# Attention and a two-layer MLP on one core: two jobs with P in float32 in place of four, four x blocks by TensorE in place of two, and products planned behind the landing

## The chip, the core and the metric

The program runs on one core of a Trainium2 chip. The metric is its time on the device in microseconds (us): 715.67 for the kernel before, the median of three runs (715.53 to 716.65). The core has TensorE (PE; its weight loads are shown apart as PEld), VectorE (DVE), ScalarE (ACT), GpSimd (POOL), and SyncE (SP), whose queue issues the DMAs here. Each engine takes its own instructions strictly in the order in which they were written down, and waits on semaphores for the others.

## The reference

Attention with pooled queries, whose output goes as tokens through a two-layer MLP (cut to what matters):

```python
# q, k, v: (4, 8, 1152, 64); w_in: (512, 2048); w_out: (2048, 512); float32
q_pool = q.reshape(B, H, S // 2, 2, D).mean(axis=3)            # 576 queries
scores = (1.0 / np.sqrt(D)) * np.matmul(q_pool, k.transpose(0, 1, 3, 2))
scores = scores - np.max(scores, axis=-1, keepdims=True)
attn = np.exp(scores)
attn = attn / (np.sum(attn, axis=-1, keepdims=True) + 1e-09)
x = np.matmul(attn, v)                       # tokens: (2304, 512) after the heads are joined
h = x @ w_in
g = h * (1.0 / (1.0 + np.exp(-h)))
return (g @ w_out).astype(np.float32)
```

## The kernel before

*Jobs.* The 32 heads are 16 pairs, four pairs to a batch. A job is one pair and one chunk of 128 queries; the 64 queries left over of two pairs make one job too. That gives 72 jobs, counted here from 0; each has two sides, one per head. Jobs 0 to 3 are the first chunk of the first four pairs. The first four pairs keep q and k in float32 (18 jobs); for the others each operand is split into two float16 halves, high and low, and a product is three: high by high, high by low, low by high.

*One job.* PE makes the scores into the PSUM tiles S0 and S1, one pair of them for all jobs, so that the next job's scores wait until both exponentials have read them (`scores`). For each side DVE takes the row maximum (L786, L793) and ACT the exponential P with its sum (L802). The usual way on: a cast to the high half (ACT or DVE, tile `phl`), the low half by a subtraction (DVE or POOL, L434), and a transpose of each half by DMA through SP's queue into `pt` (L829). Then PE multiplies P and V: 27 products a side into `po` (L937), and DVE divides by the sum into `x32` (L1009).

*Sides with P in float32* (`by_32`, the first `SIDES32` sides, so jobs 0 to 3): PE transposes P itself by nine transposes a side into PSUM (L879), ACT or DVE copies it out (L689), and the product is taken in float32 (`po<-ld,pt`, L925: 9 matmuls a side, two passes each). There is no split of P and no DMA. A third way, not used before, is `turn` (`by_pe`): the same nine transposes, then a copy to the high half and a subtraction on DVE to the low half, both out of PSUM, and products in float16.

*Token blocks.* When the four pairs of a chunk are done, `rows` turns x into columns: a split and a DMA transpose, or, for the first `X_BY_PE` blocks, four PE transposes (L1066) and a copy and a subtraction out of PSUM. 18 blocks of 128 tokens go through the MLP: 192 first products of 128 columns (L1132), tanh on ACT, gate on DVE, split on ACT and POOL, 48 second products of 512 columns (L1227; L1180 in the last block), and a store.

*Weights.* They arrive in float64 and are turned into two float16 halves in 32 pieces while the first jobs run: per piece one ACT step L608, a step on bits (L615 on ACT or L621 on DVE), a join on DVE (L636), casts and a subtraction (tiles `w1`, `w2`).

*What sets the order.* A planner (`Plan.order`) runs before anything is emitted. It steps through a model of the five queues with a cost for each operation, takes for a free engine the ready operation with the smallest number (job number plus a term from the tables `PRI`, `PRE`, `W`, `EV`), and holds back what has no tile free. `ready_at` says when an operation's inputs are there. The order that comes out is fixed in the program. Spare matmuls on a constant (`spin`, L1277) are put into gaps of PE at the start.

Of the kernel before, what the change touches and what calls it, by code (L numbers as in the profile page):

```python
# [50 lines left out]
W_OUT_SCALE = 2.0**8  # L51
SUM_GUARD = 1e-9 * math.exp(P_SHIFT)

WAIT = 0.2
AHEAD, SWITCH, STEAL = 5.072, 896.315, 0.782
PREP_LEAD = -3.124
FIRST_LEAD, FIRST_STEP = 5.48, 7.653
W_FIRST, W_STEP, W2_LATER = -3.911, 1.281, -1.06
V_LATER, V_FIRST = 1231.981, 5959.774
PRI = dict(  # L60
    score=-4011.901, top=0.206, exp=-0.93, hi=4.18, lo=0.019, turn=-5.094, flip=8248.55,
    flat=-82.007, sums=-470.427, rows=-218.032, side=0.01, load=-11.832, raw=-5.743,
    xturn=-4252.055,
)
PRE = dict(
    score=-50.801, top=-4.429, exp=1.476, hi=2.474, lo=-45.251, turn=-8.317, sums=-24.354,
    side=-5.025,
)
W = dict(
    t=1.782, low=2.528, put=-72655.385, more=3.2, hi=-5.024, lo=-4.185,  # L70
)
EV = dict(
    x=12.863, xh=12.347, xl=35.706, px=23.928, tanh=-54.817, gate=-8.882, ghi=-226.385, glo=-20.279,
    osb=8.238,
)
SOON = 8
BUFS = dict(w=1, slots=4, b=13, m=17, x4=1, small=3, S=1, mm=2)
# [1 line left out]
SPARE_B = 1  # L79
RAW_ROOM, LOAD_ROOM, P32_ROOM, PHL_ROOM = 2, 4, 1, 1  # L80
PIECES = 4, 2
BOTH_BY_PE, ONE_BY_PE, EVERY = 0, 0, 99


F32_PAIRS = 4
# [16 lines left out]
MORE = True  # L102
SUM_BY_PE = False
VC = D + 2 if SUM_BY_PE else D
X_BY_PE = 2
SIDES32 = 8
LAST = B * FULL + B // 2 - 1


# [33 lines left out]
class Plan:  # L143
# [29 lines left out]
    def ready_at(self, op, engine):  # L173
        at = 0.0
        for b in op.before:
            same = b.engine == engine and engine not in ("dve", "dma")
            at = max(at, b.end + (0.0 if same else LATENCY[b.engine]))
        return at + (DMA_START if engine == "dma" else 0.0)

    def order(self):  # L180
# [162 lines left out]
def dve_cost(n, fast=False):  # L343
    return 0.06 + n * (0.00053 if fast else 0.00105)
# [18 lines left out]
def tile_kernel(tc, q, k, v, w_in, w_out, out):  # L363
    nc = tc.nc
    with ExitStack() as ctx:
# [76 lines left out]
        low, high = slice(0, 64), slice(64, 128)  # L442
# [109 lines left out]
        def weights(n):  # L552
# [67 lines left out]
            def low_on(engine):  # L620
# [4 lines left out]

            ways = {
                "act": ("act", act_cost(512) + 0.02, low_act),
                "dve": ("dve", dve_cost(512, True), low_on(nc.vector)),
            }
            either(  # L630
                [ways[x] for x in LOW_BY],
# [311 lines left out]
        def finish(j):  # L943
# [15 lines left out]
            for i, (pp, col) in enumerate(sides(j)):  # L959
                pt = st["pt"][i]  # L960
                keep = col * P
                if ch is None:
                    hs, parts = (0, 1), ((low, (low, high)[i]), (high, (high, low)[i]))
                else:
                    hs, parts = (col,), ((whole, whole),)
                tokens = [x for n in range(2) for x in pt_tokens(j, n)]
                if by_32(j, i):
                    add(
                        "pe", 9 * 4 * pe_cost(64) + 0.1,
                        lambda pt=pt, pp=pp, hs=hs, keep=keep: heads(  # L970
                            po(), whole32(pt), None, hs, None, keep, v32s[pp]()
                        ),
                        j + pri(j, "sums"), [*tokens, ("ld", pp, "v")],
                        [("po", j)], [po, pt, v32s[pp], x32], matmuls=18,
                    )
                    continue
                add(
                    "pe", 0.787 if len(hs) == 1 else 0.86,
                    lambda pt=pt, pp=pp, hs=hs, parts=parts, keep=keep: heads(
                        po(), pt(), vt[pp](), hs, parts, keep  # L980
                    ),
                    j + pri(j, "sums"), [*tokens, ("vh", pp), ("vl", pp), ("one", pp)],
                    [("po", j)], [po, pt, vt[pp], x32], matmuls=27 * len(hs), mode=0 if len(hs) == 1 else 2,
                )
# [349 lines left out]
```

## Time and profile before

| | us |
|---|---|
| median of 3 runs | 715.67 |
| the profiled execution | 716.49 |
| its span | 714.7 |
| PE busy | 678.1 (95%) |
| DVE busy | 553.0 (77%) |
| ACT busy | 464.9 (65%) |
| POOL busy | 304.3 (43%) |

The profile is one execution; its span leaves out 1.79 us around it. Busy shares are means over stages that have different limits, so they are read by stage. Matmuls are pipelined: a group's mean time of one is longer than the distance between two, so PE's costs are taken from rows that show a run of them from start to start. On ACT and DVE neighbouring rows overlap by about a tenth of a microsecond.

### The profile page before, as it was taken

Reading aid. Unit: us, or ns where it says so; the run is one execution under the profiler, and the core shown is the slowest. Engines: PE = TensorE matmul, PEld = TensorE weight load, DVE = VectorE, ACT = ScalarE, POOL = GpSimd, SP = SyncE. Lnnn points to the kernel's source line nnn. Section 1 sums busy time; section 2 is a strip of 40 time slices with the busy share of each in tenths; the row PEclk is TensorE's granted clock in tenths of the full one; section 3 lists DMA queues with packets and bytes.
Section 4 is the critical chain, followed back from the end, with each engine's and each line's share of the span. In section 5 each row is a group of like instructions: output and inputs, shape, how many; then the busy total and the mean of one; then the engine's idle time right before and its main releaser. Section 6 shows DMA issues by size and latency. Waiting matters only on the chain.

```text
span 714.7 us, 23377 instructions
## 1 busy us (share of the span) xinstructions
PE 678.1 (95%) x10128; PEld 492.2 (69%) x10128; DVE 553.0 (77%) x903; ACT 464.9 (65%) x691; POOL 304.3 (43%) x204
## 2 busy tenths in 40 slices
PE   7898879999999999999999999999999999999997
PEld 5666546767656685858576777675867676868767
DVE  5777969898888988988769887779978887895111
ACT  4788887876776665667566667577757675665221
POOL 1637657746727021366420516164544052404111
PEclk9999999999999999999999999999999999999999
DMA  8983799999999998999999899999999999999000
GB/s 344 412 342 72 143 212 198 202 239 215 222 242 193 183 178 153 174 220 200 213 263 159 152 175 178 169 248 202 197 240 191 184 161 187 164 155 160 24 17 16
DMA packets 353416, 135.75 MB, mean 190 GB/s; under 512 B 340641, under 2 KB 340897, under 8 KB 353313
## 3 DMA queue, kind: packets, MB, share of 16 engines
q1 hardware_dynamic: 353152, 134.13, 97.4%
q8 instruction: 79, 1.29, 0.8%
q14 instruction: 25, 0.20, 0.1%
q10 hardware_dynamic: 160, 0.13, 0.1%
HBM read 45.09 MB, written 4.72 MB: 70 GB/s over the span
## 4 chain that ended last, share of the span: by engine, by line
PE 37%; DMA 10%; DVE 9%; ACT 6%; issue 3%; SPq 1%; POOL 0%; ACTq 0%; DVEq 0%
PE mm L1132 14%; PE mm L1227 9%; DMA pt<-phl 8%; PE po L937 7%; PE S L725 6%; DVE nm L786 4%; DVE phl L434 3%; ACT phl L410 2%; ACT p L802 2%; DMA ld<-q 2%; PE mm L1180 1%; ACT t L1146 1%; DMA ld<-v 1%; DMA xt<-xs 0%; DVE t L1153 0%
## 5 line engine op out<-in xcount | busy, mean ns | idle before, releaser
L802 ACT ACTIVATE p<-S,nm 128x1152 f32<-128x1152 f32 x144 | 175.2, 1217 | 93.6 <-DVE nm L793 68.8
L1132 PE MATMUL mm<-xt,w 128*128 128x128 f16 x3456 | 203.0, 219 | 5.0 <-DMA xt<-xs 1.4
L786 DVE TENSOR_REDUCE nm<-S 128x1 f32<-128x1152 f32 x144 | 194.0, 1347 | 14.7 <-PE S L725 14.6
L1132 PEld LDWEIGHTS <-w 128*128 128x128 f16 x3456 | 194.7, 98 | 11.4 <-issue 3.8
L1227 PE MATMUL mm<-w,g 128*128 128x512 f16 x816 | 186.1, 379 | 1.6 <-DVE nm L793 1.0
L434 POOL TENSOR_TENSOR g<-t,g 128x512 f16<-128x512 f32 x71 | 94.0, 1325 | 216.2 <-ACT g L410 187.0
L434 DVE TENSOR_TENSOR phl<-p,phl 128x1152 f16<-128x1152 f32 x96 | 145.5, 1522 | 19.0 <-ACT phl L410 15.3
L725 PE MATMUL S<-K,Q 64*128 64x512 f16 (+7 forms) x1320 | 136.6, 366 | 0.5 <-ACT p L802 0.3
L1227 PEld LDWEIGHTS <-g 128*128 128x128 f16 x816 | 75.9, 98 | 86.0 <-issue 1.2
L937 PE MATMUL po<-V,pt 128*128 128x64 f16 (+1 forms) x4104 | 124.0, 194 | 11.2 <-DMA pt<-phl 6.2
L937 PEld LDWEIGHTS <-pt 128*128 128x128 f16 (+1 forms) x4104 | 115.8, 101 | 23.8 <-issue 8.5
L434 POOL TENSOR_TENSOR phl<-p,phl 128x1152 f16<-128x1152 f32 x40 | 98.0, 2450 | 55.5 <-ACT phl L410 39.0
L410 ACT ACTIVATE phl<-p 128x1152 f16<-128x1152 f32 x85 | 98.3, 1161 | 4.5 <-DMA pt<-phl 2.8
L1153 DVE SCALAR_TENSOR_TENSOR t<-t,mm 128x512 f32<-128x512 f32 x72 | 49.1, 683 | 51.9 <-ACT t L1146 51.3
L725 PEld LDWEIGHTS <-Q 64*128 64x128 f16 (+1 forms) x1080 | 42.7, 96 | 49.4 <-issue 9.2
L1146 ACT ACTIVATE t<-mm 128x512 f32<-128x512 f32 x72 | 42.5, 591 | 24.5 <-PE mm L1132 24.2
L410 ACT ACTIVATE g<-t 128x512 f16<-128x512 f32 x69 | 43.4, 629 | 20.9 <-DVE t L1153 18.7
L414 DVE CAST phl<-p 128x1152 f16<-128x1152 f32 x51 | 43.0, 842 | 9.0 <-ACT p L802 4.3
L434 POOL TENSOR_TENSOR xs<-x,xs 128x512 f16<-128x512 f32 (+1 forms) x18 | 21.1, 1173 | 47.3 <-ACT xs L410 47.2
L725 PEld LDWEIGHTS S<-K,Q 64*128 64x128 f32 (+1 forms) x240 | 22.8, 196 | 25.0 <-issue 21.9
L1009 DVE TENSOR_TENSOR x<-po,r 128x128 f32<-128x128 f32 x72 | 20.5, 284 | 20.8 <-PE po L937 14.2
L410 ACT ACTIVATE t<-mm 128x512 f32<-128x512 f32 (+1 forms) x16 | 9.2, 578 | 30.9 <-PE mm L1227 21.1
(67 smaller groups left out, 472.9 us busy)
## 6 DMA issues: line engine op xcount, KB each, us to landing
ld<-q SPq DMA_DIRECT2D x16, 576.0 KB, 5.3
ld<-v SPq DMA_DIRECT2D x16, 576.0 KB, 5.5
ld<-k SPq DMA_DIRECT2D x12, 576.0 KB, 6.1
pt<-phl SPq DMA_TRANSPOSE x272, 4.2
wide<-w_in SPq DMA_DIRECT2D x8, 512.0 KB, 10.3
wide<-w_out SPq DMA_DIRECT2D x8, 512.0 KB, 10.7
raw<-w_in SPq DMA_DIRECT2D x8, 512.0 KB, 8.3
raw<-w_out SPq DMA_DIRECT2D x8, 512.0 KB, 7.9
```

Of the source, the lines that this page charges most:

```text
L410: nc.scalar.activation(out=out(), in_=src(), func=AF.Copy, scale=scale or 1.0)
L414: nc.vector.tensor_copy(out=out(), in_=src())
L434: return lambda: getattr(engine, op)(out=out(), in0=a(), in1=b())
L725: nc.tensor.matmul(o[to, c], lhsT=a[rows, s], rhs=x[rows, c], start=n == 0, stop=n == len(terms) - 1,)
L786: lambda: nc.vector.tensor_reduce(out=nm(), in_=ps()[:, :S], op=ALU.max, axis=AX.X),
L802: lambda: nc.scalar.activation(out=p32(), in_=ps()[:, :S], func=AF.Exp, scale=0.0625, bias=nm(), **({} if SUM_BY_PE else dict(accum_out=sm ...
L937: nc.tensor.matmul(o[to, keep : keep + n], lhsT=pt[:, hl * NK + c, cols], rhs=vv[:, at : at + n], start=c == 0 and hl + vl == 0, stop=c == ...
L1009: lambda: nc.vector.tensor_tensor(out=to(), in0=sides2()[:, :, :D], in1=r().unsqueeze(2).to_broadcast([P, 2, D]), op=ALU.mult,),
L1132: nc.tensor.matmul(o, lhsT=w[:, f // 2 % 4, wl, cols], rhs=moving(xl, kk), start=kk == 0 and wl + xl == 0, stop=kk == 3 and wl == 1,)
L1146: lambda: nc.scalar.activation(out=t(), in_=h(), func=AF.Tanh, scale=1.0 / G_SCALE),
L1153: lambda: nc.vector.scalar_tensor_tensor(out=t(), in0=t(), scalar=1.0, in1=h(), op0=ALU.add, op1=ALU.mult,),
L1227: nc.tensor.matmul(o(), lhsT=g[ff // 4]()[:, gl, ff % 4], rhs=w[:, u % 4, wl, e * DM : e * DM + DM], start=ff == ffs[0] and gl + wl == 0, ...
```

## The change

The float32 way is kept for jobs 0 and 1 alone (`SIDES32` 8 to 4). Of jobs 2 and 3 the second side goes the way of `turn` (`ONE_BY_PE` 0 to 4; the float32 way has precedence in jobs 0 and 1), the first side the usual way by DMA. Four x blocks in place of two are turned by PE. In the planner an operation behind a DMA transpose becomes ready 1.648 us later (`LATE`), a float32 product side costs 2.02 us in place of 1.15, and the bit step on DVE 0.08 more. All numbers of the priority tables are new, which gives another order everywhere.

```diff
-WAIT = 0.2
-AHEAD, SWITCH, STEAL = 5.072, 896.315, 0.782
+WAIT = 0.188
+LATE = 1.648
+AHEAD, SWITCH, STEAL = 1.176, 16340.733, 0.723
...
 PRI = dict(
-    score=-4011.901, top=0.206, exp=-0.93, hi=4.18, lo=0.019, turn=-5.094, flip=8248.55,
+    score=-153567.955, top=-0.932, exp=-2.904, hi=1.21, lo=0.374, turn=82.142, flip=1360342.311,
...
-BOTH_BY_PE, ONE_BY_PE, EVERY = 0, 0, 99
+BOTH_BY_PE, ONE_BY_PE, EVERY = 0, 4, 99
...
-X_BY_PE = 2
-SIDES32 = 8
+X_BY_PE = 4
+SIDES32 = 4
...
         for b in op.before:
             same = b.engine == engine and engine not in ("dve", "dma")
-            at = max(at, b.end + (0.0 if same else LATENCY[b.engine]))
+            at = max(at, b.end + (0.0 if same else LATENCY[b.engine]) + (LATE if b.moves == "turn" else 0.0))
...
             ways = {
                 "act": ("act", act_cost(512) + 0.02, low_act),
-                "dve": ("dve", dve_cost(512, True), low_on(nc.vector)),
+                "dve": ("dve", dve_cost(512, True) + 0.08, low_on(nc.vector)),
             }
...
                 if by_32(j, i):
                     add(
-                        "pe", 9 * 4 * pe_cost(64) + 0.1,
+                        "pe", 2.02,
```

PE, from the scores of job 1 to those of job 2, before (the last number of a name counts tiles; `p32_30` and `p32_35` are P of job 0, `p32_57` is of job 1, `S0_75` takes job 2's scores):

```order
L725 MATMUL S1_41_225<-K_8_105,Q_26_177 128x128
L879 MATMUL pp_46_247<-one_1_84,p32_30_193 128x128
...
L879 MATMUL pp_55_278<-one_1_84,p32_35_206 128x128
...
L1277 MATMUL spin_56_281<-one_1_84 128x256
L925 MATMUL po_59_290<-ld_5_96,pt_52_269 128x64 x9
L925 MATMUL po_59_290<-ld_5_96,pt_39_222 128x64 x9
L879 MATMUL pp_64_323<-one_1_84,p32_57_287 128x128 x4
L879 MATMUL pp_71_343<-one_1_84,p32_57_287 128x128 x4
L879 MATMUL pp_74_355<-one_1_84,p32_57_287 128x128
L725 MATMUL S0_75_357<-K_38_220,Q_65_329 128x512
```

The same place now, as far as job 3's scores (`p32_32` and `p32_37` are of job 0, `p32_55` and `p32_60` of job 1, `p32_81` of job 2, `S0_65` takes job 2's scores, `S0_93` job 3's):

```order
L726 MATMUL S1_42_226<-K_8_105,Q_28_179 128x128
...
L880 MATMUL pp_53_270<-one_1_84,p32_37_208 128x128
L926 MATMUL po_57_278<-ld_5_96,pt_51_263 128x64 x9
L926 MATMUL po_57_278<-ld_5_96,pt_40_223 128x64 x9
L726 MATMUL S0_65_319<-K_17_135,Q_45_241 128x512
...
L880 MATMUL pp_71_340<-one_1_84,p32_55_275 128x128 x4
...
L880 MATMUL pp_86_390<-one_1_84,p32_60_294 128x128
L844 MATMUL pp_87_393<-one_1_84,p32_81_374 128x128 x4
L926 MATMUL po_90_402<-ld_10_112,pt_84_385 128x64 x9
L726 MATMUL S0_93_418<-K_58_289,Q_85_387 128x512
```

Job 1's transposes moved behind job 2's scores, the spin is gone, and the products of job 1 are parted by job 3's scores.

ACT, between the exponentials of job 1 and job 2, before (`mm`, `w1`, `w2` and `wide` are weights, `pt<-pp` copies of transposed P):

```order
L802 ACTIVATE p32_63_320,sum_58_288<-S0_40_224,nm_53_273 128x1152
L410 ACTIVATE w2_0_66_331<-wide_11_114 128x512
...
L608 ACTIVATE mm_72_348<-wide_11_114 128x512
...
L410 ACTIVATE w2_0_66_331<-wide_11_114 128x512
L608 ACTIVATE mm_79_371<-wide_23_166 128x512
L608 ACTIVATE mm_80_374<-wide_23_166 128x512
L615 ACTIVATE wide_23_166<-wide_23_166 128x512
L410 ACTIVATE wide_23_166<-wide_23_166 128x512
...
L410 ACTIVATE w1_0_50_261<-wide_23_166 128x512 x2
L802 ACTIVATE p32_92_428,sum_93_429<-S1_76_358,nm_84_390 128x1152
```

And now:

```order
L803 ACTIVATE p32_60_294,sum_56_276<-S0_41_225,nm_52_268 128x1152
L609 ACTIVATE mm_62_309<-wide_11_114 128x512
L616 ACTIVATE wide_11_114<-wide_11_114 128x512
L616 ACTIVATE wide_35_203<-wide_35_203 128x512
L411 ACTIVATE wide_11_114<-wide_11_114 128x512
L609 ACTIVATE mm_69_333<-wide_11_114 128x512
L411 ACTIVATE w1_0_50_261<-wide_11_114 128x512
L616 ACTIVATE wide_35_203<-wide_35_203 128x512
L690 ACTIVATE pt_75_356<-pp_71_340 128x512
L690 ACTIVATE pt_75_356<-pp_73_349 128x512
L690 ACTIVATE pt_75_356<-pp_76_359 128x128
L803 ACTIVATE p32_81_374,sum_82_375<-S1_66_320,nm_72_347 128x1152
```

Between the two exponentials stood fourteen instructions, and now ten: weight steps and three of the copies went to later places.

PE around the scores of job 65, before (`S1_1270` is job 64's, `S1_1287` job 65's; `pt_1283` and `pt_1288` hold P of job 64):

```order
L725 MATMUL S1_1270_11213<-K_1106_9585,Q_1105_9570 128x128
...
L937 MATMUL po_1274_11241<-V_1066_9208,pt_1257_11123 128x64
...
L1227 MATMUL mm_1263_11185<-w2_1_192_997,g_1255_11091 128x512
...
L725 MATMUL S1_1287_11348<-K_1147_9999,Q_1148_10026 128x128
...
L937 MATMUL po_1289_11370<-V_1081_9333,pt_1276_11304 128x64
...
L1227 MATMUL mm_1263_11185<-w2_1_192_997,g_1268_11209 128x512
...
L937 MATMUL po_1296_11452<-V_1127_9833,pt_1283_11332 128x64
```

And now (`S1_1261` is job 64's, `S1_1279` job 65's, `S1_1294` job 66's; `pt_1283` and `pt_1276` hold P of job 64):

```order
L726 MATMUL S1_1261_11211<-K_1090_9525,Q_1088_9510 128x128
...
L1133 MATMUL mm_1257_11192<-xt_1193_10567,w1_1_212_1227 128x128
...
L1228 MATMUL mm_1273_11348<-w2_0_78_364,g_1243_11031 128x512
...
L726 MATMUL S1_1279_11373<-K_1098_9602,Q_1102_9635 128x128
...
L1228 MATMUL mm_1273_11348<-w2_0_78_364,g_1258_11205 128x512
...
L938 MATMUL po_1287_11420<-V_1080_9439,pt_1267_11298 128x64
...
L726 MATMUL S1_1294_11497<-K_1014_8715,Q_1013_8713 128x128
...
L1228 MATMUL mm_1273_11348<-w2_1_238_1368,g_1265_11266 128x512
...
L938 MATMUL po_1297_11529<-V_1125_9895,pt_1283_11409 128x64
```

The product of job 64 stood behind one later job's scores, and now stands behind two.

## Rows read from the trace of the kernel before

**Rows 1.** Page, part 1: busy us (share of span), instructions of each engine.

```profile
PE 678.1 (95%) x10128; PEld 492.2 (69%) x10128; DVE 553.0 (77%) x903; ACT 464.9 (65%) x691; POOL 304.3 (43%) x204
```

**Rows 2.** Windows: stretch, length, busy (instructions) by engine, clock, DMA share, GB/s.

```profile
15.00:60.10 45.10, 40.83 (x282) 30.57 (x282) 33.19 (x68) 37.41 (x71) 21.45 (x18) 0.93 0.87 334
60.10:136.00 75.90, 64.84 (x807) 43.98 (x806) 64.29 (x107) 64.71 (x100) 52.47 (x38) 0.96 0.92 175
136.00:220.60 84.60, 79.77 (x1315) 58.56 (x1314) 74.56 (x116) 59.45 (x85) 45.75 (x29) 1.00 1.14 220
220.60:643.60 423.00, 413.97 (x6683) 297.21 (x6680) 358.30 (x576) 276.81 (x398) 163.09 (x99) 1.00 1.10 189
```

**Rows 3.** Timeline of PE, start: start us, us, operation, count [idle before it].

```profile
7.17 2.21 PE L725 MATMUL S<-K,Q 64*128 64x512 f32 x12
...
15.01 3.54 PE L725 MATMUL S<-K,Q 64*128 64x512 f32 x12
...
21.15 4.13 PE L925 MATMUL po<-ld,pt 128*128 128x64 f32 x36
...
31.67 1.09 PE L879 MATMUL pp<-one,p 128*128 128x128 f32 x8
...
59.50 0.66 PE L1066 MATMUL px<-one,x 128*128 128x128 f32 x4
...
86.50 1.75 PE L937 MATMUL po<-V,pt 128*128 128x64 f16 x54
```

**Rows 4.** Timeline of PE, end of the run.

```profile
668.70 10.88 PE L1132 MATMUL mm<-xt,w 128*128 128x128 f16 x192
679.42 10.52 PE L1227 MATMUL mm<-w,g 128*128 128x512 f16 x48
```

**Rows 5.** Groups by form: count | busy us, mean ns | idle before.

```profile
L434 DVE TENSOR_TENSOR phl<-p,phl 128x1152 f16<-128x1152 f32 x96 | 145.5, 1522 | 19.0 <-ACT phl L410 15.3 <-issue 0.9 <-DMA pt<-phl 0.8
...
L410 ACT ACTIVATE phl<-p 128x1152 f16<-128x1152 f32 x85 | 98.3, 1161 | 4.5 <-DMA pt<-phl 2.8
L434 POOL TENSOR_TENSOR phl<-p,phl 128x1152 f16<-128x1152 f32 x40 | 98.0, 2450 | 55.5 <-ACT phl L410 39.0 <-DVE phl L414 16.5
...
L608 ACT ACTIVATE mm<-raw 128x512 f32<-128x512 f32 x16 | 10.0, 630 | 1.5 <-DVE raw L636 1.3
...
L689 ACT ACTIVATE pt<-pp 128x512 f32<-128x512 f32 x16 | 9.0, 598 | 5.8 <-PE pp L879 5.8
...
L410 ACT ACTIVATE w<-raw 128x512 f16<-128x512 f32 x13 | 8.8, 677 | 4.3 <-DVE raw L636 3.9 <-POOL raw L419 0.2
...
L689 ACT ACTIVATE pt<-pp 128x128 f32<-128x128 f32 x8 | 2.2, 279 | 1.1 <-PE pp L879 1.1
...
L1087 DVE TENSOR_TENSOR xt<-px,xt 128x512 f16<-128x512 f32 x2 | 1.4, 686 | 0.0
```

**Rows 6.** Waits of PE, 136.0 to 643.6 us: us in total, times, longest.

```profile
PE po L937 <- DMA pt<-phl: 6.2, 13, 1.1
PE mm L1132 <- DMA xt<-xs: 1.4, 1, 1.4
PE mm L1132 <- DVE x L1009: 1.3, 1, 1.3
```

**Rows 7.** Timeline of PE around the scores of job 65.

```profile
588.29 1.64 PE L725 MATMUL S<-K,Q 64*128 64x512 f16 x18
...
596.08 1.64 PE L725 MATMUL S<-K,Q 64*128 64x512 f16 x18
...
601.82 1.67 PE L937 MATMUL po<-V,pt 128*128 128x64 f16 x45
603.83 0.44 PE L937 MATMUL po<-V,pt 128*128 128x64 f16 x9 [0.34 <-DMA pt<-phl]
```

**Rows 8.** Windows of 2.5 us around the scores at 27.84 us.

```profile
25.00:27.50 2.50, 1.32 (x11) 0.90 (x10) 0.75 (x2) 1.71 (x3) 1.53 (x2) 1.00 1.02 407
27.50:30.00 2.50, 2.42 (x7) 1.22 (x9) 2.46 (x4) 2.08 (x6) 1.15 (x1) 0.60 1.02 413
```

More of the change, by code (lines that the diff above doesn't have):

```diff
@@ L52 @@
 SUM_GUARD = 1e-9 * math.exp(P_SHIFT)
-WAIT = 0.2
-AHEAD, SWITCH, STEAL = 5.072, 896.315, 0.782
[L56 to L59, printed above, removed]
+WAIT = 0.188
+LATE = 1.648
+AHEAD, SWITCH, STEAL = 1.176, 16340.733, 0.723
+PREP_LEAD = 3.414
+FIRST_LEAD, FIRST_STEP = -1.033, 4.348
+W_FIRST, W_STEP, W2_LATER = 1.745, 0.381, 0.127
+V_LATER, V_FIRST = -21.728, 920.607
 PRI = dict(
-    score=-4011.901, top=0.206, exp=-0.93, hi=4.18, lo=0.019, turn=-5.094, flip=8248.55,
-    flat=-82.007, sums=-470.427, rows=-218.032, side=0.01, load=-11.832, raw=-5.743,
-    xturn=-4252.055,
+    score=-153567.955, top=-0.932, exp=-2.904, hi=1.21, lo=0.374, turn=82.142, flip=1360342.311,
+    flat=-594.16, sums=-261.869, rows=77822.173, side=-0.112, load=-7.42, raw=0.435,
+    xturn=-1745.766,
 )
 PRE = dict(
-    score=-50.801, top=-4.429, exp=1.476, hi=2.474, lo=-45.251, turn=-8.317, sums=-24.354,
-    side=-5.025,
+    score=-275.636, top=2.096, exp=-576.815, hi=-129.112, lo=-0.155, turn=-90.803, sums=30.874,
+    side=-0.473,
 )
 W = dict(
-    t=1.782, low=2.528, put=-72655.385, more=3.2, hi=-5.024, lo=-4.185,
+    t=-0.485, low=-0.247, put=-52091.624, more=-0.135, hi=0.278, lo=0.045,
 )
 EV = dict(
-    x=12.863, xh=12.347, xl=35.706, px=23.928, tanh=-54.817, gate=-8.882, ghi=-226.385, glo=-20.279,
-    osb=8.238,
+    x=8.92, xh=12.1, xl=30.158, px=12382.15, tanh=11.246, gate=-4.866, ghi=8.711, glo=6.93,
+    osb=13.174,
 )
```

## The prediction

> **What bounds the kernel now.** I began with the page. TensorE (PE) is busy 95% of the span [rows 1], so the first guess is that its work sets the time. The windows, cut where the scores of jobs 5, 13 and 22 start (jobs count from 0), say where that holds [rows 2]. From 220.6 to 643.6 us PE is busy 413.97 of 423.00 us: bound by its work. From 136.0 to 220.6 us it is 79.77 of 84.60, with VectorE (DVE) at 74.56 close behind. From 15.0 to 136.0 us it is not the bound alone: PE leaves 4.27 + 11.06 us idle, and ScalarE (ACT) is busy 37.41 of 45.10 and 64.71 of 75.90 us, that is 83% and 85%. There four engines pass each job round in a ring: scores on PE, maximum on DVE, exponential on ACT, transposes on PE, copies on ACT, products on PE, while the weights are converted on the same ACT and DVE. After 643.6 us nothing but products is left.
>
> Then the waits of PE from 136.0 to 643.6 us [rows 6]: 6.2 us of its 13.9 idle (4.83 + 9.03 by [rows 2]) are products of P and V that wait for the transposing DMA, 13 times, at most 1.1. The next, 1.4 and 1.3 us, are single. PE's rows at one such place [rows 7]: the scores of job 65 start at 596.08, 45 of the 54 products of job 64 stand at 601.82, and the last 9 sit 0.34 us for the transposed low half.
>
> **The change part by part.**
>
> *PE's work.* A job with P in float32 costs 4.13 us for its 18 products, 36 passes; one with P in two halves costs 1.75 for 54 [rows 3]. Two jobs go over: -2 x (4.13 - 1.75) = -4.8 us. Transposes: 8 sides of 9 become 6 sides of 9, 18 fewer, at 1.09 us for 8: -2.5. Two x blocks more by PE at 0.66 each: +1.3. Sum -6.0 us, all before 220 us. All else of PE's useful work is the same in number. The score filler (spin) falls from 112 to 104 matmuls; it stands in idle time and counts nothing.
>
> *ACT and DVE at the start.* Up to the second exponential of job 5 the new order of ACT has 7 weight steps L608 fewer, 9 casts to w1 and w2 fewer, 6 copies out of a transpose fewer, one step of the first token block (two instructions) fewer, and 2 more casts of P and 3 more L615: by the means [rows 5] -7 x 0.63 - 9 x 0.68 - (4 x 0.60 + 2 x 0.28) - 1.2 + 2 x 1.16 + 3 x 0.68 = -10.3 us, where L615 is priced like a cast of the same 512 columns. Consecutive rows overlap by about a tenth, so -9. DVE's list there is equal within 1 us: it loses 10 bit steps and 4 joins of weights and gains two sums of q, one rest and 6 low halves out of PSUM, which I price by the one like them, 0.69 for 512 columns [rows 5], so 2 x 0.69 + 0.28 = 1.7 a side. PE also has less in the way: the scores of job 2 no longer stand behind job 1's transposes. If ACT binds and stays as full as it is, 83%, job 5 comes 9 / 0.83 = 11 us earlier; if the ring's latency binds, only what PE loses there is gained, about 3.
>
> From job 5 to 13 the postponed weights come back: the new list is 2.4 us longer on ACT and 2.7 on DVE. At 85% that is +3. So the scores of job 13 start 11 - 3 = 8 us earlier at best by ACT, 0 by the ring. I take 6; the list is closer to the first.
>
> *What that lead costs.* It is bought with token-block work not yet done. Before the scores of job 13 PE's order now holds 24 of the second products (L1227) where it held 60, and two of the four x blocks by PE are still to come: 36 x 0.219 = 7.9 (10.52 us for 48 [rows 4]), + 1.3. That 9.2 us comes later, where PE is the bound. First products (L1132) are equal in number there. At the end it shows: after the last scores 48 first products and 21 second ones more remain, 48 x 0.056 (192 take 10.72, from start to start) + 21 x 0.219 = 7.3 us.
>
> *Products later.* The planner adds 1.648 us to a landing before it places what waits for it. By the order, with PE's durations, the work between the end of a job's scores and its product was 11.8 us at the least over jobs 10 to 69 (median 15.8) and is now 13.6 (16.6). At the place shown it grows from 11.8 to 15.4, against some 14 needed (589.9, the end of job 64's scores, to 603.8). So nearly all 13 waits go: -6.2. Bounds: 0, if other waits stand behind them; -8, if the single waits of 1.4 and 1.3 us were luck too and part of them goes. I take -6, nearest to the row. The cover of the longer way is the MLP work between. More is in flight at a time, in tiles of pool b whose number is unchanged.
>
> *Rests on GpSimd.* The reordering moves low halves of P from DVE to POOL: 96 and 40 become 79 and 59. One takes 2.45 us there and 1.52 on DVE [rows 5], so 19 sides land 0.9 later, which the 1.6 more room covers; if not, 19 x 0.9 would be exposed in part. SP gets four more transposes of P and two fewer of x. DVE gains 17 x 1.52 = 26 us of room over the whole run, off the bound.
>
> *TensorE's clock.* It was granted in full at 25.0 to 27.5 us with 1.32 us of PE busy, and fell to 0.60 in the window behind it [rows 8]; the scores at 15.01 took 3.54 us, those at 7.17 only 2.21 [rows 3]. Between the scores of jobs 1 and 4 the old order has a spin ahead of each job's products; the new one has none, and 41 transposes. The Trainium skill (TensorE: Matmul & The Clock Gate, Part 4: PE-mode transpose) says that transposes do not count as busy for the clock. By that rule the scores of jobs 2 to 4 would run at the lower clock, and the time would be that of the fourth rival below. The trace is undecided: the fall at 27.5 us follows transposes, but a wait too.
>
> **The sum.** -6 (job 13 starts earlier) + 9.2 (work postponed beyond it) - 6 (waits for the landing) = -2.8. The 6.0 us of PE work saved lie inside the first term and are not counted again. The profiled execution took 716.49 us, 1.79 more than its span of 714.7; 716.5 - 2.8 = 713.7. The median of the runs is 0.8 lower than that execution, so against it 712.9. Since the gain of the start may reach 8 and the waits 8, I say 712, with 709 to 714 for this case.
>
> **The rivals.**
> 1. *The lead is not real (slower).* The ring of the first 13 jobs is bound by scores, maximum, exponential and by DVE, which carries 2.7 us more from job 5 to 13 and 4.2 us more from 13 to 21, in the stretch where it is busy 88% [rows 2]. Then job 13 starts 1 us earlier instead of 6, 9.2 us are still postponed, and DVE costs another 2 of its 4.2; the landing gives 6 back: -1 + 9.2 + 2 - 6 = +4.2, 720. It decides where job 13 starts less than 2 us earlier. For it: DVE at 64.29 of 75.90 is as full as ACT. Against it: DVE sits below ACT to 60 us, where the list is cut most.
> 2. *The waits change owner (same).* PE's order is fixed; a product that no longer waits lets the next matmul meet its own wait, on DVE or the scores' two buffers [rows 6]. Of the 6 us 3 stay: -6 + 9.2 - 3 = +0.2, 715.9.
> 3. *Both gains in full.* Job 13 starts 10 us earlier and 8 of the waits go: -10 + 9.2 - 8 = -8.8, 706.9. The order is tighter on PE early than ACT's list needs, which speaks for it; DVE's against.
> 4. *The clock falls in the transposes.* Three score blocks at the lower clock cost 3 x (3.54 - 2.21) = 4.0 us of the lead: -2 + 9.2 - 6 = +1.2, 716.9.
>
> **How the numbers follow.** Chances: forecast 0.38, rival 1 0.23, rival 2 0.18, rival 3 0.16, rival 4 0.05. Less than 0.2% (1.4 us) cannot be told from no change. Faster than 714.2: all of rival 3 and nearly all of the forecast, 0.53. Within 714.2 to 717.1: rival 2 and parts of the forecast and of 4, 0.21. Slower: rival 1 and the rest of 4, 0.26. The range reaches from 704.5, beyond rival 3, to 719.5, just short of rival 1's centre.
>
> **What would show it.** The scores of job 5 start some 9 to 11 us earlier than 60.1 and those of job 13 some 6 earlier than 136.0. PE's waits of products for the transposing DMA fall from 6.2 to under 1.5 us, and idle time of PE between job 22 and the last scores from 9 to some 4. The last scores start 8 to 12 us earlier than 643.6, and the tail behind them is 78 us instead of 71.1. It is wrong if job 13 starts no earlier, if PE's waits only change name, or if the granted clock between 25 and 60 us is well under 0.93.

## The result and the profile after

The changed kernel is slower: a median of 719.68 us over 20 runs against 715.21 over 20 runs of before on the same chip, ratio 1.0058 (95% interval 1.0032 to 1.0085). On a second chip (12 and 24 runs) it was 716.67 against 713.71, ratio 1.003 (1.0002 to 1.0059). Ratios, here and below, are of means, without the few slow runs that lie over 1.5% above the fastest of their kernel. 712 was predicted. The profiled execution took 722.74 us, its span is 721.0.

The page's part 1 of after, which answers to [rows 1] (busy us, share, instructions):

```profile
PE 670.7 (93%) x10146; PEld 485.9 (67%) x10146; DVE 528.0 (73%) x894; ACT 476.9 (66%) x699; POOL 322.0 (45%) x209
```

PE is busy 7.4 us less and the span is 6.3 longer. Windows of after, cut at the scores of jobs 5, 13, 22 and 71 as in [rows 2] (stretch, length, busy by engine from PE on, granted clock, DMA share, GB/s):

```profile
15.40:54.00 38.60, 32.08 (x226) 22.96 (x226) 29.70 (x56) 29.64 (x55) 13.23 (x13) 0.87 0.99 326
54.00:130.50 76.50, 57.56 (x847) 42.23 (x846) 68.45 (x117) 61.11 (x99) 47.07 (x32) 1.00 0.97 178
130.50:225.00 94.50, 85.93 (x1285) 59.45 (x1287) 75.50 (x130) 71.50 (x103) 50.50 (x33) 0.98 1.13 229
225.00:642.60 417.60, 407.88 (x6680) 293.77 (x6678) 330.63 (x557) 286.55 (x404) 191.44 (x111) 1.00 1.09 190
642.60:721.00 78.40, 74.75 (x1042) 58.74 (x1041) 17.25 (x27) 23.02 (x37) 16.78 (x15) 1.00 0.29 52
```

Job 5 starts at 54.0 (60.1 before), job 13 at 130.5 (136.0), but job 22 at 225.0 (220.6) and the last scores at 642.6 (643.6). The tail is 78.4. In the first row the clock is 0.87, where [rows 2] had 0.93.

PE's waits from 136.0 to 643.6 us in after (us in total, times, longest), beside [rows 6]:

```profile
PE S L726 <- ACT p L803: 4.3, 4, 2.1
PE po L938 <- DMA pt<-phl: 3.8, 5, 1.9
PE mm L1133 <- DVE t L1154: 2.7, 5, 1.7
PE mm L1228 <- DVE t L1154: 1.2, 2, 0.7
PE mm L1228 <- DVE nm L794: 1.2, 3, 0.5
```

The products wait 3.8 us for the landing, not 6.2. The scores wait 4.3 us for the exponential (0.3 before), and first and second products stand behind DVE.

PE's timeline of after where the clock is low (start, us, operation, count, [idle before]):

```profile
26.04 0.66 PE L880 MATMUL pp<-one,p 128*128 128x128 f32 x4
26.96 0.66 PE L880 MATMUL pp<-one,p 128*128 128x128 f32 x4 [0.26 <-DVE wide L637]
28.20 0.33 PE L880 MATMUL pp<-one,p 128*128 128x128 f32 x1 [0.58 <-ACT pt L690]
28.69 1.09 PE L880 MATMUL pp<-one,p 128*128 128x128 f32 x8 [0.16 <-ACT pt L690]
30.59 0.33 PE L880 MATMUL pp<-one,p 128*128 128x128 f32 x1 [0.81 <-ACT pt L690]
31.07 1.03 PE L844 MATMUL pp<-one,p 128*128 128x128 f32 x4 [0.16 <-ACT pt L690]
31.90 3.94 PE L926 MATMUL po<-ld,pt 128*128 128x64 f32 x18
35.77 3.31 PE L726 MATMUL S<-K,Q 64*128 64x512 f32 x12
39.01 2.22 PE L926 MATMUL po<-ld,pt 128*128 128x64 f32 x18
...
44.81 3.90 PE L726 MATMUL S<-K,Q 64*128 64x512 f32 x12
```

For six microseconds PE has nothing but transposes with short waits between them. The 18 product passes behind, one side of job 1, take 3.94 us, the 18 of its other side at 39.01 only 2.22, and the scores of jobs 3 and 4 take 3.31 and 3.90 where 2.21 is full speed [rows 3]. Excess: 1.72 + 1.10 + 1.69 = 4.5 us. The windows of 2.5 us agree:

```profile
27.00:29.50 2.50, 1.76 (x12) 1.33 (x13) 2.47 (x3) 2.50 (x5) 2.42 (x3) 1.00 1.02 412
29.50:32.00 2.50, 1.54 (x9) 1.11 (x8) 1.29 (x4) 2.50 (x6) 0.37 (x1) 0.84 1.02 408
32.00:34.50 2.50, 2.50 (x14) 2.50 (x14) 1.97 (x5) 1.52 (x5) 0.00 (x0) 0.50 1.02 406
34.50:37.00 2.50, 2.50 (x11) 1.87 (x12) 1.03 (x2) 2.50 (x5) 1.30 (x1) 0.50 1.03 410
```

The clock is at its upper level (2.4 GHz) to 29.5 us, and at the lower one (0.50, 1.2 GHz) from 32 to 37, while PE is busy throughout.

### The profile page after: what moved, and what is told of

It reads as the page before. It is cut to its first block, busy times and chain, and to the rows that moved or that the text cites. A ratio compares the mean times of both kernels' runs of the same rounds, so it can differ in the third digit from the quotient of the medians.

```text
span 721.0 us, 23444 instructions
## 1 busy us (share of the span) xinstructions
PE 670.7 (93%) x10146; PEld 485.9 (67%) x10146; DVE 528.0 (73%) x894; ACT 476.9 (66%) x699; POOL 322.0 (45%) x209
## 5 line engine op out<-in xcount | busy, mean ns | idle before, releaser
L435 POOL TENSOR_TENSOR phl<-p,phl 128x1152 f16<-128x1152 f32 x59 | 143.7, 2438 | 80.8 <-DVE phl L415 52.3
L726 PE MATMUL S<-K,Q 64*128 64x512 f16 (+7 forms) x1320 | 132.4, 363 | 9.3 <-ACT p L803 8.9
L435 DVE TENSOR_TENSOR phl<-p,phl 128x1152 f16<-128x1152 f32 x79 | 112.5, 1428 | 34.5 <-ACT phl L411 32.4
L411 ACT ACTIVATE phl<-p 128x1152 f16<-128x1152 f32 x102 | 118.2, 1161 | 7.3 <-issue 3.1
L435 POOL TENSOR_TENSOR xs<-x,xs 128x512 f16<-128x512 f32 (+1 forms) x14 | 16.9, 1204 | 70.6 <-ACT xs L411 70.6
L411 ACT ACTIVATE g<-t 128x512 f16<-128x512 f32 x61 | 38.2, 628 | 14.2 <-DVE t L1154 14.1
L726 PEld LDWEIGHTS S<-K,Q 64*128 64x128 f32 (+1 forms) x240 | 20.1, 186 | 28.2 <-issue 20.0
L415 DVE CAST phl<-p 128x1152 f16<-128x1152 f32 x36 | 28.8, 800 | 4.4 <-ACT p L803 2.4
L538 DVE SCALAR_TENSOR_TENSOR V<-ld,V 128x1152 f16<-128x1152 f32 x16 | 22.4, 1400 | 12.0 <-ACT V L411 11.9
L411 ACT ACTIVATE V<-ld 128x1152 f16<-128x1152 f32 x13 | 15.1, 1162 | 22.1 <-DMA ld<-v 22.1
```

The source lines that it names most:

```text
L411: nc.scalar.activation(out=out(), in_=src(), func=AF.Copy, scale=scale or 1.0)
L415: nc.vector.tensor_copy(out=out(), in_=src())
L435: return lambda: getattr(engine, op)(out=out(), in0=a(), in1=b())
L538: lambda: nc.vector.scalar_tensor_tensor(out=values(1), in0=v3(), scalar=V_SCALE, in1=values(0)[:, :, :D], op0=ALU.mult, op1=ALU.subtract,),
L726: nc.tensor.matmul(o[to, c], lhsT=a[rows, s], rhs=x[rows, c], start=n == 0, stop=n == len(terms) - 1,)
```

## The experiments

Three theories were set against each other, with some rivals that the expectations name. *Q*: steps at the heads of ACT's and DVE's queues wait for loads and hold maximum, exponential and the next scores. *The landing*: what the later products are worth by themselves. *K*: TensorE's clock. A fourth, *B* in the expectations, is that whatever is held longer in a buffer stops what wants its place. To move single instructions without a new plan, `later` takes the planner's finished list, adds `by(op)` us to the planned start of chosen instructions and sorts the list again, with all dependencies kept; in the first four runs nothing else moved, from the fifth on whatever needs the same buffers moves along. Ratios are to before on the same chip, with 95% intervals.

**The landing alone, and the counts alone.**

```diff
 # products_later: before; products_earlier: after, with -1.648; products_later_b: as the first, buffers moved along
+        order = later(order, capacity, by)  # by(op): 1.648 for po and x of jobs >= 8, else 0.0
 # late_only: before
+            at = max(at, b.end + (...) + (1.648 if b.moves == "turn" else 0.0))
 # counts_only: before
-ONE_BY_PE = 0; X_BY_PE = 2; SIDES32 = 8
+ONE_BY_PE = 4; X_BY_PE = 4; SIDES32 = 4
```

> The kernel before with its order kept, except that the products of P and V of jobs 8 and later, and the step that scales them, stand 1.648 us of planned time later: the one part of the change that was to save the waits for the landing, by itself. As the prediction has it: product waits after 136 us fall from 6.2 to under 1.5 us and the time falls 5 to 6 us, ratio 0.992 to 0.993. Rival (waits change owner): the product waits fall as much, but waits of other matmuls behind DVE, ACT or the scores' buffers rise by nearly the same, and the ratio is 0.997 to 1.001.

> The changed kernel with its order kept, except that the products of P and V of jobs 8 and later stand 1.648 us of planned time earlier, so this part of the change is undone by itself. If the later products save 6 us in it as predicted: product waits rise from 3.8 to 9 or 10 us and the time by 5 to 6, ratio 1.013. If the waits only change owner: within 1.5 us of the changed kernel, 1.004 to 1.008. If the later products cost something by themselves: faster than the changed kernel, below 1.004.

> The kernel before, its planned order kept, with the products of P and V of jobs 8 and later and the step that scales them 1.648 us of planned time later, and what needs their buffers moved along. As predicted for this part: ratio 0.992 to 0.993 and product waits below 1.5 us. Waits change owner: 0.997 to 1.001. Theory B (later products hold tiles of pool b and PSUM tiles longer, and the exponentials, transposes and other matmuls wait for those): slower, 1.005 to 1.03, with the product waits gone or not.

> The kernel before with nothing changed but the planner's 1.648 us behind a landing; the planner lays out the whole order anew. As predicted for this part: ratio 0.992 to 0.993. Waits change owner: 0.997 to 1.001. Theory B: over 1.003, since the planner itself puts exponentials later where a product holds its buffers longer; the product waits fall all the same.

> The kernel before with nothing changed but the counts: two jobs with P in float32 in place of four, jobs 0 to 3 with one side by TensorE's transposes, four x blocks by TensorE in place of two; planned anew with the planner's numbers of before. By the prediction's count PE has 6.0 us less to do before 220 us. If that is worth itself: ratio 0.992 to 0.996. If the first jobs are bound by ACT and DVE instead, to which the sides give more sums and halves: 1.000 to 1.006. If the numbers of the planner only fit one set of counts: over 1.006.

| | median us | ratio |
|---|---|---|
| products_later | 736.95 | 1.0332 (1.0298 to 1.0366) |
| products_earlier | 740.95 | 1.0384 (1.0346 to 1.0421) |
| products_later_b | 733.77 | 1.0305 (1.0264 to 1.0347) |
| late_only | 737.94 | 1.0374 (1.0331 to 1.0416) |
| counts_only | 728.82 | 1.022 (1.0173 to 1.0267) |

PE's waits in products_later_b from 137 to 660 us:

```profile
PE mm L1198 <- DVE x L1075: 8.0, 7, 2.9
PE mm L1198 <- DVE t L1219: 5.4, 5, 1.8
PE S L791 <- ACT p L868: 2.2, 4, 1.0
PE mm L1293 <- DVE x L1075: 1.9, 2, 1.5
```

The product waits for the landing are gone altogether (6.2 to 0; 0.6 in late_only), as that run's expectation has it and further than in after, and nothing is gained by it: 9.9 us of first and second products now stand behind the step that scales the later product (`x`), and 5.4 behind the gate. The waits changed owner. But every one of the five is 15 to 27 us slower than before, whichever way it moves the products, so their times do not price the part moved; the control below shows that reordering by itself can cost as much. counts_only came out as its third expectation has it (over 1.006): a planner whose numbers fit one set of counts lays out another one badly, so this run does not price the 6.0 us of PE's work saved either.

**Queue heads.** In after the casts of V wait longer on ACT than anything else does for a load. Group of the page (mean ns of one, idle before):

```profile
L411 ACT ACTIVATE V<-ld 128x1152 f16<-128x1152 f32 x13 | 15.1, 1162 | 22.1 <-DMA ld<-v 22.1
```

One such place, ACT, DVE and PE in after's timeline:

```profile
204.30 1.64 PE L726 MATMUL S<-K,Q 64*128 64x512 f16 x18
...
206.83 1.16 ACT L411 ACTIVATE V<-ld 128x1152 f16<-128x1152 f32 x1 [1.83 <-DMA ld<-v]
...
208.03 1.36 DVE L538 SCALAR_TENSOR_TENSOR V<-ld,V 128x1152 f16<-128x1152 f32 x1 [1.42 <-ACT V L411]
...
209.97 1.35 DVE L787 TENSOR_REDUCE nm<-S 128x1 f32<-128x1152 f32 x1
...
215.55 1.04 PE L726 MATMUL S<-K,Q 64*128 64x512 f16 x4 [2.06 <-ACT p L803]
```

The maximum of job 20 begins 4 us after its scores have ended, and the next scores wait 2.06 us.

```diff
+        order = later(order, capacity, by)
 # v_later: 5.0 for every split of V          v_later_b: the same for pairs 4 and later
 # v7_later: 5.0 for the split of V of pair 7
 # weights_later: 2.0 for every weight step   w26_later: 5.5 for the steps of block 26
 # loads_earlier: -3.0 for every load
```

> The changed kernel with its order kept, except that the casts and rests that split V stand 5 us of planned time later in the lists of ACT and DVE; their first readers come 11 us and more behind. Theory Q (queue heads: since the change all 13 casts of V on ACT stand where the load of V is planned to land, and a load that lands later holds ACT and DVE, and with them maximum, exponential and the next scores): ACT's idle time before V casts falls from 22.1 to under 8 us, PE's waits of scores for ACT's exponential after 130 us from 4.5 to under 1.5, job 22 starts 3 us or more earlier than 224.97, and the time is 3 to 4 us below the changed kernel, a ratio to before of 1.001 to 1.003. Rival W (the postponed weight steps hold the queues): no change, 1.005 to 1.007. Rival C (only the granted clock differs): no change either, 1.005 to 1.007, and the runs spread with their clock.

> The changed kernel with its order kept, except that every step which converts weights (ACT, DVE, GpSimd) stands 2 us of planned time later in the lists; PE's list is the same. Theory W (weight steps wait at the heads of DVE and ACT for loads that land late, 3.79 us at 132.8 us): the wait at 132.8 us goes and the time is 2 to 3 us below the changed kernel, ratio 1.002 to 1.003. Theory Q with V alone: within 1 us of the changed kernel, 1.004 to 1.007. A third way: PE's products of weights now wait longer for the steps, and it gets slower, over 1.008.

> The changed kernel, its planned order kept, with the casts and rests that split V of pairs 4 and later 5 us of planned time later in the lists of ACT and DVE, where what needs the buffers that they read moves along; the start up to job 12 is the changed kernel's. Theory Q (V's splits at the heads of ACT and DVE wait for loads and hold the next scores): ACT's idle time before V casts falls by 8 us or more, PE's waits of scores for the exponential after 130 us go from 4.5 to under 1.5, ratio to before 1.000 to 1.003. Theory B (buffers: the first try lost 22 us because whatever is held longer in pool b stops the exponentials or loads that want its place): slower than the changed kernel again, 1.008 or more, with DMA's share lower after 225 us. Theory C (clock): 1.004 to 1.007.

> The changed kernel with a single pair moved: the cast and the rest that split V of pair 7 go behind the work of job 20's maximum and exponential, three rows down in ACT's list and some five in DVE's; nothing else moves. Theory Q (a step at a queue's head that waits for a load holds the ring): the maximum of job 20 starts 1.5 to 3 us earlier after its scores, job 21 follows job 20 by 9 us in place of 11.25, no wait of 2 us ahead of its scores, no fall of the clock there, and the whole time falls by 1.5 to 3.5 us. If the gap only moves on (the order of all that follows is fixed, and other waits catch it): job 21 is earlier, the last scores are not, time within 1 us of the changed kernel.

> The changed kernel with a single weight block moved: the steps that convert block 26 go 5.5 us of planned time later, so that DVE's bit step no longer stands ahead of job 13's maximum; 2 rows of ACT, 3 of DVE, 1 of GpSimd move, and job 14's scores move past 6 second products. Theory Q with the weights: the 3.79 us wait of DVE for the load and the 2.1 us wait of PE at 132.7 us go, job 14 starts 2 to 3 us earlier after job 13 (12.2 us now), and the time falls by 1 to 3 us. If another load is waited for at the next head: job 14 no earlier, time within 1 us.

> The changed kernel with every load of Q, K, V and of weights 3 us of planned time earlier in the list of the DMA queue where its buffer is free; the lists of PE, ACT, DVE and GpSimd are the changed kernel's. Theory Q: the idle time of ACT before V casts falls from 22.1 to under 12, that of DVE for raw and wide blocks falls too, and the time falls 2 to 5 us. Theory B (buffers of pool b are what loads wait for; a load that is issued earlier sits at the head of the queue for its buffer and holds the transposes behind it): slower, by 3 us or more, with product waits for the landing up from 3.8.

| | median us | ratio |
|---|---|---|
| v_later | 746.62 | 1.0456 (1.0423 to 1.049) |
| weights_later | 743.76 | 1.0398 (1.0353 to 1.0443) |
| v_later_b | 733.6 | 1.0296 (1.0261 to 1.0332) |
| v7_later | 720.1 | 1.0081 (1.005 to 1.0111) |
| w26_later | 720.67 | 1.0088 (1.0052 to 1.0124) |
| loads_earlier | 723.22 | 1.0111 (1.0066 to 1.0155) |

In v_later_b ACT's idle time before V casts fell from 22.1 to 6.3 us, as Q wants, and the kernel was 2.4% slower than after (1.0296 against 1.0058). In v7_later, with two instructions moved, job 21 follows job 20 after 10.4 us in place of 11.25, but the next product waits 2.6 us for the gate and job 23 comes 29.3 us behind job 20, in after 27.4. In w26_later the wait of 2.14 us is gone and one of 2.22 stands 7 us further on. So Q is not borne out: the waits are real, but none of the six runs that took some away gained time. It is not excluded either, since each of the six may have paid the price of a reordering that the control below shows. The same holds for B: loads_earlier came out as B has it (slower, product waits 7.3 us in place of 3.8), and so did v_later_b (DMA's share 1.06 from 225 to 640 us in place of 1.09), but nothing tells this from the cost of reordering. weights_later came out by its third way (over 1.008).

**A control.** Before, with 0 to 0.5 us added to every planned start, a different number for each instruction:

```diff
+        order = later(order, capacity, lambda op: op.n * 7919 % 1000 / 1000 * 0.5)
```

> The kernel before with up to 0.5 us added to each planned start, a different amount for every instruction, and nothing meant by it: 14 rows of ACT and 164 of DVE change, PE's list is the same. If reordering by itself costs what the first tries lost: ratio 1.005 to 1.03. If only what was moved in them cost it: 0.998 to 1.003.

740.94 us, ratio 1.0343 (1.029 to 1.0396). A reordering of DVE and ACT that means nothing costs as much as the ones that meant something. Its waits of PE from 137 to 659 us:

```profile
PE po L1003 <- DVE t L1219: 4.6, 7, 1.4
PE S L791 <- ACT p L868: 3.6, 8, 0.8
PE mm L1198 <- DVE x L1075: 3.0, 2, 1.5
PE mm L1198 <- DVE nm L859: 2.7, 4, 1.0
PE po L1003 <- DMA pt<-phl: 2.5, 4, 0.9
```

Even here the product waits fall, from 6.2 to 2.5 us, and the kernel is 25 us slower. The control moved 178 rows, some of the runs above only a few, so it gives no price for a single move; but no gain of single moves can be read from the runs above as long as the price of leaving a tuned order is unknown. What is left to test is what can be tried with the order kept.

**The clock.** First the changed kernel again, for the clock of single runs; then matmuls that do no work, written into a tile which the transposes behind them overwrite. All lists but PE's stay as they are.

```diff
 # spin4: after; spin2: two; spin4_job1: four, j == 1 alone; before_spin4: the same in before
                 def transposes(c=c, m=m, ps=ps):
+                    x = one().bitcast(F16)
+                    for _ in range(4 if j in (1, 2, 3) else 0):
+                        nc.tensor.matmul(ps()[:, :256], lhsT=x[:, :P], rhs=x, start=True, stop=True)
                     for a in range(m):
 # more_transposes: after, in place of the matmul
+                        nc.tensor.transpose(ps()[:, :P], p32()[:, :P], one())
```

> The changed kernel once more, beside the three that follow, for the granted clock of single runs. If the clock makes the difference: the time of a run falls by about 0.6 us for each 0.001 of mean granted clock, and the runs at 0.994 and above lie at 715 to 718 us. If the order alone makes it: no relation, and every run about 1.003 to 1.008 of before.

> The changed kernel with four idle matmuls (128x256, 16 bit, into the tile that the transposes then overwrite) ahead of each group of transposes of jobs 1 to 3, 48 in all; everything else is as it was. Theory K (the clock falls because PE does nothing but transposes and short waits from 26 to 32 us): the granted clock from 25 to 55 us rises from 0.5 to 0.7 in the low windows to over 0.9, the 18 products at 31.9 us take 2.1 us in place of 3.94 and the scores of jobs 3 and 4 take 2.2 in place of 3.3 to 4.2; that gives back 4.8 to 6.8 us, the idle matmuls cost 2 to 4 of them, job 5 starts 1 to 3 us earlier than 53.97, mean clock 0.995 or more, ratio to before 0.998 to 1.001. Theory P (the order of the ring sets the time, the clock only goes along): the idle matmuls come on top, job 5 starts 3 to 5 us later, ratio 1.008 to 1.012.

> The same with two idle matmuls ahead of each group, 24 in all. Theory K: if half of it is enough for the clock, the cost is 1 to 2 us and the ratio 0.997 to 1.000; if not, the low windows stay and the ratio is 1.004 to 1.007. Theory P: 1.005 to 1.009.

> The kernel before with four idle matmuls ahead of each group of transposes of jobs 1 to 3, 72 in all. Its low windows before 60 us cost 3.4 us, and some of its transposes lie next to spins and products already. Theory K: the scores of job 2 take 2.2 us in place of 3.90, gain 1.7 to 3.4 us less 3 to 5 for the idle matmuls, ratio 1.000 to 1.004. Theory P: 1.004 to 1.010.

> The changed kernel with four more transposes (128x128, float32, about 0.11 us each, the same length as an idle matmul at the full clock) ahead of each group of jobs 1 to 3, 48 in all, into the tile that the group then overwrites. If only the kind of work counts (by the Trainium skill, TensorE: Matmul & The Clock Gate, Part 4: PE-mode transpose, transposes do not count as busy for the clock): the clock falls between 27 and 36 us as in the changed kernel, the 18 products behind take 3.9 us again, job 5 starts 3 to 5 us later than 53.97, ratio 1.007 to 1.012. If any busy PE keeps its clock: as with the idle matmuls, products 2.1 us, job 5 at 50 to 52, ratio 0.993 to 0.999.

> The changed kernel with four idle matmuls ahead of each group of transposes of job 1 alone, 24 in all. If the fall at 27 to 36 us begins there and the later one (45 us) follows from its own transposes: products at 32 us take 2.1 us, scores of job 3 2.2, scores of job 4 still 3.3 to 4.2; job 5 at 51.5 to 53, ratio 0.997 to 1.001. If the second fall only follows from the first: as spin4, job 5 at 50 to 51, ratio 0.992 to 0.996.

In the runs of after_again (12) and of before beside it (23) the time follows the run's mean clock: 1177.3 - 465.5 x clock (correlation -0.79) and 1088.6 - 376.5 x clock (-0.60), fitted. At a clock of 0.992 that is 715.5 and 715.1: no difference clear of the scatter. The mean clock is 0.9900 and 0.9946, and that 0.0046 by the two slopes is 1.7 to 2.1 of the 2.3 us between the two means (716.4 and 714.1). On the first chip this cannot be said: the 20 runs of after have a mean clock of 0.9882 and by their own fit 718.0 us at 0.992, and the clocks of before beside them are not on record.

| | median us | ratio | mean clock of its runs (of before beside it) | clock lost before 60 us |
|---|---|---|---|---|
| before | 715.21 | 1 | | 3.4 |
| after | 719.68 | 1.0058 (1.0032 to 1.0085) | 0.9882 (not on record) | 5.1 |
| after_again | 716.67 | 1.003 (1.0002 to 1.0059) | 0.9900 (0.9946) | 8.55 |
| spin4 | 711.56 | 0.9941 (0.991 to 0.9973) | 0.9977 (0.9920) | 0 |
| spin2 | 713.38 | 0.9965 (0.9934 to 0.9996) | 0.9940 (0.9920) | 1.7 |
| more_transposes | 711.04 | 0.996 (0.9934 to 0.9986) | 0.9978 (0.9947) | 0 |
| spin4_job1 | 713.59 | 1.0 (0.9982 to 1.0018) | 0.9929 (0.9947) | 3.4 |
| before_spin4 | 721.22 | 1.01 (1.0062 to 1.0137) | 0.9924 (0.9920) | 0 |

(Last column, us: (1 - granted clock) x 5, summed over the 5 us windows of the one profiled run.) The place of the low clock, in spin4:

```profile
30.80 0.60 PE L884 MATMUL pp<-one 128*128 128x256 f16 x4 [0.31 <-ACT pt L690]
31.23 0.27 PE L886 MATMUL pp<-one,p 128*128 128x128 f32 x1
31.34 0.60 PE L845 MATMUL pp<-one 128*128 128x256 f16 x4
31.77 0.60 PE L847 MATMUL pp<-one,p 128*128 128x128 f32 x4
32.21 2.12 PE L932 MATMUL po<-ld,pt 128*128 128x64 f32 x18
34.26 2.21 PE L726 MATMUL S<-K,Q 64*128 64x512 f32 x12
...
42.58 2.21 PE L726 MATMUL S<-K,Q 64*128 64x512 f32 x12
```

Products and scores are back at full speed. The 48 matmuls more (0.44 us for four, from start to start: 5.3 us) make the kernel 6 to 8 us faster than after (0.9941 against 1.003 and 1.0058; 5 to 7 in more_transposes), and spin4 beats both kernels. The rows and the clock are as K expects, and the ratio lies even below the 0.998 to 1.001 expected; the clock is a cause and not only a companion. spin4_job1 shows two places: with job 1's transposes fed the products at 31.96 us take 2.22, but the scores of job 4 still 3.12, and job 5's 3.90. And in more_transposes:

```profile
31.29 0.27 PE L884 MATMUL pp<-one,p 128*128 128x128 f32 x1
31.40 0.60 PE L844 MATMUL pp<-one,p 128*128 128x128 f32 x4
31.83 0.60 PE L846 MATMUL pp<-one,p 128*128 128x128 f32 x4
32.27 2.12 PE L930 MATMUL po<-ld,pt 128*128 128x64 f32 x18
34.32 2.21 PE L726 MATMUL S<-K,Q 64*128 64x512 f32 x12
```

Transposes do it as well as matmuls. So it was not the kind of work that let the clock fall: here PE does nothing but transposes from 25.02 to 32.27 us and keeps its clock. The Trainium skill (TensorE: Matmul & The Clock Gate, Part 4: PE-mode transpose) says that transposes do not count as busy in the same way. For these float32 transposes, which the trace lists as matmuls, the measurement says otherwise. What differs between after and these two is how busy PE was kept between the transposes: from 27.0 to 32.0 us it was busy 1.76 + 1.54 of 5.00 in after, 2.35 + 2.19 in more_transposes, 2.30 + 2.19 in spin4.

That does not settle it, though. By their traces, six profiled executions ran the same instructions in the same order on every engine up to 97 us: after, after_again, products_earlier, w26_later, loads_earlier and v7_later. In five of them the clock is down to 0.50 from 32.0 to 34.5 us, and job 5 starts at 53.70 to 55.68. In v7_later PE did the same transposes with nearly the same gaps (the second row has 1.53 busy where after has 1.54), and the clock held at first:

```profile
27.00:29.50 2.50, 1.76 (x13) 1.20 (x11) 2.43 (x4) 2.50 (x5) 2.42 (x3) 1.00 1.02 412
29.50:32.00 2.50, 1.53 (x12) 1.24 (x12) 1.14 (x3) 2.50 (x6) 0.19 (x1) 1.00 1.02 407
32.00:34.50 2.50, 2.50 (x20) 1.96 (x21) 2.14 (x5) 1.54 (x5) 0.00 (x0) 1.00 1.03 413
```

Its 18 product passes take 2.12 us and job 3's scores 2.21, the clock falls first at job 4's scores (3.15), and job 5 starts at 50.37. So the fall behind these transposes comes in most executions and not in all, and with no instruction before job 5 changed it goes with a job 5 that is 3.3 to 5.3 us later (0.2 to 0.5 of that stands already at job 2's scores). One profiled run therefore does not show that a cure works; the mean clocks over 12 and more runs do (0.9977 and 0.9978 against 0.9882 and 0.9900).

before_spin4 is 1% slower, which is what theory P expected of it (1.004 to 1.010). Its one profiled run lost no clock before 60 us, but over its seven runs the mean clock is 0.9924, where before beside it has 0.9920: there the 72 matmuls gave no clock back. What costs these 5 us is not shown, since the profiled run is the fastest of the seven (716.95) and has job 5 at 61.70 in place of 60.09, but the last scores at 643.27 in place of 643.61.

## Why the prediction was wrong

Starts of jobs in the profiled runs (us):

| | before | after | after_again | spin4 | more_transposes |
|---|---|---|---|---|---|
| job 5 | 60.09 | 53.97 | 55.68 | 50.80 | 50.91 |
| job 13 | 136.04 | 130.47 | 132.64 | 125.45 | 125.09 |
| job 14 | 145.22 | 142.66 | 143.02 | 134.88 | 134.47 |
| job 22 | 220.65 | 224.97 | 222.50 | 213.73 | 213.81 |
| job 71 | 643.61 | 642.61 | 641.14 | 634.10 | 635.06 |
| end of span | 714.7 | 721.0 | 719.5 | 712.5 | 713.4 |

*The start (-6).* Job 13 came 5.6 us earlier (3.4 in after_again): the size was about right, the way to it was not. Job 5 was to come 9 to 11 earlier and came 6.1 earlier, with 4.5 us of slow rows in between. With the clock kept, spin4 has job 5 9.3 and job 13 10.6 earlier, which was the upper end of that step (rival 3).

*The work postponed (+9.2).* Right where it could be seen: the tail is 78.4 us (78 predicted).

*The landing (-6).* This is the first step that failed: "So nearly all 13 waits go: -6.2", which was taken as time. In the six profiled runs that keep the changed order (the four above, spin2 and spin4_job1) products wait 1.9 to 5.5 us for the landing from job 13 on, where under 1.5 was predicted, and in after the 3.8 that are left all lie behind 225 us. More to the point, PE's idle time from job 13 to the last scores did not fall by 6: it is 12.7 to 18.3 us in these runs, 13.9 before. In after it is 8.57 + 9.72 = 18.3: the scores wait 4.3 us for the exponential, and first and second products for DVE. That stretch takes 507.6 us before, 512.1 in after and 504.1 to 510.0 in the others, and the sum wants 4.1 less than before (9.2 - 7.3 of work postponed, less 6); only spin2 comes near that, with 3.5. In the profiled run of after this one term is 8.7 us off, nearly all that the sum is. It is what rival 2 (the waits change owner, 0.18) says, though that rival let 3 of the 6 us stay. Why the landing is still waited for is open.

*The clock.* The second step that failed: the sum has no term for the clock in the first 60 us, and rival 4, with its 4.0 us for three score blocks, was given 0.05. Rows of after give 4.5 us (one side of job 1's products and the scores of jobs 3 and 4), after_again lost more, and over many runs the mean clock is 0.9882 and 0.9900. It was held to be undecided because the only rule at hand was one on transposes; the rows [rows 8] showed the plainer thing, a clock that falls behind a stretch with idle gaps, and the new order has more of such a stretch in it: the spins went out (no spin from job 1 to job 4) and waits on copies out of PSUM stand between the transposes.

*The sum.* With the clock kept, the time is 0.9941 (0.991 to 0.9973) or 0.996 (0.9934 to 0.9986) of before; the forecast of -2.8 us is 0.9961. That is no merit of the working: a larger gain of the start stood in for the landing, which gave nothing, and before beside these runs had the lower clock. At some 460 us per unit of mean clock, between the slopes fitted, that alone is 2.6 of the 4.7 us between the means of spin4 and before, and 1.4 of 2.6 in more_transposes. Rival 1's 720 is the forecast nearest to the 719.68 measured, but by luck: it wanted job 13 less than 2 us earlier, and 5.6 was measured.

*Open.* The stretch from job 13 to 22 takes 84.6 us before, 94.5 in after, 89.9 in after_again, 88.3 in spin4 and 88.7 in more_transposes, with the same lists on ACT and DVE in the last four. It does not go with the clock lost before 60 us, of which after_again lost the most. In spin4 the DVE step at job 13's maximum waits 1.13 us for its load, in after 3.79; what sets this was not settled. Why the order of before loses 25 us by a jitter of half a microsecond is not explained beyond the waits shown; nor can what the later products are worth inside an order made for them be measured by moving them out of it.

## What to carry to other kernels

Look at the granted clock of every stretch where PE waits in small bits for another engine, in more than one execution, and price the rows behind it at the lower level; work that only keeps PE busy there can pay for itself, but only where it raises the clock of the runs (in before it did not, and cost 1%). A wait that is last on PE is not time to be gained until one knows what stands behind it in each queue. And move instructions of a tuned order one at a time beside a control that moves them for no reason: here the control cost more than most effects sought.

## What the runs showed of the hardware

Extra float32 transposes held the clock as well as extra float16 matmuls did (mean clock of 12 runs each 0.9978 and 0.9977, against 0.9900 without them). The same instructions with nearly the same gaps (PE busy 3.28 to 3.37 of 5.00 us from 27 to 32 us) were followed by the lower clock in five profiled executions and by the full clock in one. A run's time moved by some 310 to 620 us per unit of mean granted clock (fits of after, after_again and three sets of before, 12 to 23 runs each); in spin2 and spin4_job1 no such relation is clear (correlation -0.23 and -0.16). Runs of after_again, one program on one chip, ranged from 0.983 to 0.995 (712.33 to 721.24 us): a comparison of medians within 1% needs the clocks of the runs beside it.
